# Reading the moving operand of every full-chunk product with its two halves in turn

## The chip, the cores and the metric

The kernel runs on one core of one Trainium2 chip. The metric is the device time of one execution in microseconds (us). Five engines work side by side and meet at semaphores: TensorE (PE in the rows, its loads of the stationary operand PEld), VectorE (DVE), ScalarE (ACT), GpSimd (POOL) and SyncE (SP), which here issues nearly all DMAs.

## What is computed

`x` is 4 batches of 12544 tokens with 128 channels, `inducing` has 32 rows. Two attention steps follow each other, then a maxout layer without bias:

```python
def mab(q, kv):
    s = scale * (q @ kv.transpose(0, 2, 1))
    s = s - s.max(-1, keepdims=True)
    a = np.exp(s)
    a /= a.sum(-1, keepdims=True) + 1e-09
    return a @ kv
h = mab(I, x)           # 32 rows per batch
y = mab(x, h)           # 12544 rows per batch, then as one list of tokens
h2 = np.maximum(np.maximum(y @ w1, y @ w2), y @ w3)   # 768 wide
out = h2 @ w_out
```

## The kernel before

**What a product is.** The second attention has only 32 rows of `h` per batch, so the kernel multiplies the weights with these rows first. The tile `us` holds, for a batch, `h` times (w1 - w2), `h` times (w3 - w2), and `h` times w2 times w_out, each as a high and a low part, on 128 rows. What remains for each token is the 32 probabilities, which stand in the tile `pT`, also as high and low parts on 128 rows, one column for a token. The maximum of the three branches is then the w2 branch plus max(relu(u), v), and the w2 branch goes through `us` straight to the output.

**Chunks and slots.** A batch has 98 tiles of 128 tokens: one short group of 2 tiles and six groups of 16. A full group is cut into four full chunks of 512 tokens, the short group is one chunk of 256. So there are 24 full chunks and one short chunk in a batch, 96 and 4 in all. A chunk has six slots, one for each block of 128 of the 768 hidden channels: 600 slots. A slot issues these products on TensorE, all of 128 rows by 128 stationary columns, with 512 moving columns in a full chunk, of type fp32r (four bytes a column, written by the engine that rounds it):

- line 778: `pu` from `us` and `pT`; line 784: `pv` from `us` and `pT` (stage 1, in `advance`),
- lines 846, 847, 848: three products into `acc` from `hi`, `hi` and `lows`, with `wo_hi`, `wo_lo`, `wo_hi` (stage 2),
- at the chunk's first slot also line 845: `us` and `pT` straight into `acc`.

Between the stages, ScalarE writes `ru` = relu(`pu`) (line 793), VectorE writes `h` = max(`pv`, `ru`) (line 814), ScalarE rounds it to `hi` (line 803), and GpSimd, for four or five of 24 slots VectorE, writes the rest `lows` = `h` - `hi` (lines 811, 817). Stage 2 of a slot runs six slots behind its stage 1 (`LAG`). `pu` and `pv` have two PSUM banks each, so the product of `pu` in slot s+1 waits until `ru` of slot s-1 has been read out. After the sixth slot ScalarE copies `acc` to `o` (line 859), and SP writes it out.

**The order around it.** Everything is issued by hand, in the order of the program. A full group is a window of 24 slots. At fixed slots of a window the kernel issues bursts of other products (scores of the next group at line 684, the first attention of the next batch at lines 366 and 502) and the steps of `scores_steps`, which make the probabilities of the next group: the last two write `ph` (ScalarE, line 730) and `pl` (VectorE, line 733) at slots 14 and 15. `probs` then issues, two chunks ahead, four DMAs (line 759) that bring 32 rows each of `ph` and `pl` into `pT`. The first chunks of batch 0 get `pT` by two products with `turn` instead (line 753).

Of the kernel before, what the change touches and what calls it, by code (L numbers as in the profile page):

```python
# [8 lines left out]
F32 = mybir.dt.float32  # L9
# [16 lines left out]
def kernel(ctx, tc, x, xt, ind_t, w1, w2, w3, w_out, out):  # L26
    nc = tc.nc
    B, N, C = x.shape
    M = ind_t.shape[1]
    DF = w1.shape[1]  # L30
    P = 128
    NT = N // P
    NJ = DF // P
# [158 lines left out]
    def first_load(what):  # L192
# [12 lines left out]
        out=sel[:, :M], in_=ident.rearrange("p (q m) -> p m q", m=M), axis=AX.X, op=ALU.add  # L205
    )
    nc.vector.tensor_copy(
        out=sel[:, M:].rearrange("p (q m) -> p q m", m=M),
        in_=sel[:, :M].unsqueeze(1).to_broadcast([P, NQ - 1, M]),
# [17 lines left out]
    wo_hi = const.tile([P, NJ, C], F32R, name="wo_hi")  # L227
    wo_lo = const.tile([P, NJ, C], F32R, name="wo_lo")
# [54 lines left out]
    def row_of(j):  # L283

        return 2 * (j % (NJ // 2)) + j // (NJ // 2)
# [32 lines left out]
    state = {}  # L318
# [355 lines left out]

    def scores_products(b, gi, bank):
        nt = groups[gi]["nt"]
        w = nt * M
        st = state[b]  # L680
        xT = st["xT"].pop(gi)
        sp = bank
        for q in range(NQ):
            nc.tensor.matmul(  # L684
                out=sp[q * M : (q + 1) * M, :w], lhsT=st["hT"][:, :M], rhs=xT[:, q * w : (q + 1) * w], start=True, stop=True
            )
        st["s"][gi] = sp

    def scores_steps(b, gi):

        nt = groups[gi]["nt"]
        w = nt * M
        st = state[b]
        sp = st["s"].pop(gi)
        flat = sp[:, :w]
        ev = flat.rearrange("p (t m) -> p t m", m=M)
        nc.vector.transpose(out=flat, in_=flat)
        yield
        mx = wk.tile([P, GT], F32, name="mx", tag="mx")
        nc.vector.tensor_reduce(out=mx[:, :nt], in_=ev, axis=AX.X, op=ALU.max)  # L700
        yield
        nc.vector.tensor_sub(out=ev, in0=ev, in1=mx[:, :nt].unsqueeze(2).to_broadcast([P, nt, M]))
        yield
        nc.scalar.activation(out=flat, in_=flat, func=AF.Exp, scale=scale)
        yield
        rs = wk.tile([P, GT], F32, name="rs", tag="rs")
        nc.vector.tensor_reduce(out=rs[:, :nt], in_=ev, axis=AX.X, op=ALU.add)
        yield
        if b == 0 and gi < 2:
            nc.vector.tensor_scalar_add(out=rs[:, :nt], in0=rs[:, :nt], scalar1=1e-9)  # L710
        else:
            nc.scalar.activation(out=rs[:, :nt], in_=rs[:, :nt], func=AF.Identity, bias=eps)
        yield
        nc.vector.reciprocal(out=rs[:, :nt], in_=rs[:, :nt])
        nc.vector.tensor_mul(out=ev, in0=ev, in1=rs[:, :nt].unsqueeze(2).to_broadcast([P, nt, M]))
        yield
        if nt < GT:

            pn = wk.tile([P, nt, 2, 2, M], F32R, name="pn", tag="pn", bufs=1)
            e4 = ev.unsqueeze(2).to_broadcast([P, nt, 2, M])  # L720
            nc.scalar.copy(out=pn[:, :, :, 0, :], in_=e4)
            yield
            nc.vector.tensor_sub(out=pn[:, :, :, 1, :], in0=e4, in1=pn.bitcast(F32)[:, :, :, 0, :])
            st[("p", gi)] = pn
            yield
            return
        nc.vector.transpose(out=flat, in_=flat)
        yield
        ph = wk.tile([P, 512], F32R, name="ph", tag="ph")
        nc.scalar.copy(out=ph, in_=flat)  # L730
        yield
        pl = wk.tile([P, 512], F32R, name="pl", tag="pl")
        nc.vector.tensor_sub(out=pl, in0=flat, in1=ph.bitcast(F32))
        st[("p", gi)] = (ph.bitcast(F32), pl.bitcast(F32))
        yield

# [34 lines left out]
    def advance():  # L771

        s = pipe["next"]
        pipe["next"] += 1
        if s + 1 < len(slots):
            c, j = slots[s + 1]
            pu, w = bank_u[(s + 1) % 2], c.w
            nc.tensor.matmul(  # L778
                out=pu[:, :w], lhsT=state[c.b]["us"][:, 2 * j * P : (2 * j + 1) * P], rhs=c.pT[:, :w], start=True, stop=True
            )  # L780
        if 0 <= s < len(slots):
            d, j = slots[s]
            pv = bank_v[s % 2]
            nc.tensor.matmul(  # L784
                out=pv[:, : d.w],
                lhsT=state[d.b]["us"][:, (2 * j + 1) * P : (2 * j + 2) * P],
                rhs=d.pT[:, : d.w],
                start=True,
                stop=True,
            )  # L790
        if s + 1 < len(slots):
            ru = hp.tile([P, 512], F32, name="ru", tag="ru", bufs=3)
            nc.scalar.activation(out=ru[:, :w], in_=pu[:, :w], func=AF.Relu)  # L793
            relus[s + 1] = ru
        low = pipe.pop("low", None)
        if 0 <= s - 1 < len(slots):
            c, j = slots[s - 1]
            h = sums.pop(s - 1)
            hi = hp.tile([P, 512], F32R, name="hi", tag="hi", bufs=10)
            if s - 1 in HIVEC:  # L800
                nc.vector.tensor_copy(out=hi[:, : c.w], in_=h[:, : c.w])
            else:
                nc.scalar.copy(out=hi[:, : c.w], in_=h[:, : c.w])  # L803
            lo = lows[:, (s - 1) % NL, :]
            c.hh.append(hi)
            c.hl.append(lo)
            args = dict(out=lo[:, : c.w], in0=h[:, : c.w], in1=hi.bitcast(F32)[:, : c.w])
            if c.low(j):
                pipe["low"] = args
            else:  # L810
                nc.gpsimd.tensor_sub(**args)  # L811
        if 0 <= s < len(slots):
            h = hp.tile([P, 512], F32, name="h", tag="h", bufs=5)
            nc.vector.tensor_max(out=h[:, : d.w], in0=pv[:, : d.w], in1=relus.pop(s)[:, : d.w])  # L814
            sums[s] = h
        if low:
            nc.vector.tensor_sub(**low)  # L817

    class Chunk:


        def __init__(self, n, b, gi, q):
            self.n, self.b, self.gi, self.q = n, b, gi, q
            self.w = GT * M if q is not None else groups[gi]["nt"] * P
            self.hh, self.hl = [], []

        def low(self, k):
# [7 lines left out]
    def stage2(c, j):  # L835
        us = state[c.b]["us"]
        w = c.w
        if j == 0:
            c.acc = [(bank_o[c.n % 2], slice(0, w))]
            if c.n == len(chunks) - 1:  # L840
                c.acc = [(bank_a[k], slice(k * w // 2, (k + 1) * w // 2)) for k in range(2)]
        for acc, cs in c.acc:
            to = acc[:, : cs.stop - cs.start]
            if j == 0:
                nc.tensor.matmul(out=to, lhsT=us[:, 2 * DF :], rhs=c.pT[:, cs], start=True, stop=False)  # L845
            nc.tensor.matmul(out=to, lhsT=wo_hi[:, row_of(j), :], rhs=c.hh[j][:, cs], start=False, stop=False)  # L846
            nc.tensor.matmul(out=to, lhsT=wo_lo[:, row_of(j), :], rhs=c.hh[j][:, cs], start=False, stop=False)  # L847
            nc.tensor.matmul(out=to, lhsT=wo_hi[:, row_of(j), :], rhs=c.hl[j][:, cs], start=False, stop=(j == NJ - 1))  # L848

    def finish(c):  # L850
        at = groups[c.gi]["at"] + (c.q or 0) * c.w
# [18 lines left out]
    for b in range(B):  # L870
        for gi in range(NG):
            full = groups[gi]["nt"] == GT
# [57 lines left out]
    for b in range(B):  # L930
        n = b + 1
        for g in range(1, NG):
            s0 = begins(b * (NG - 1) + g)
            if g + 1 < NG:

                if n == B:

                    if g % 2:
                        burst(s0 + 2, *((scores_products, b, k, bank_a[k % 2]) for k in (g + 1, g + 2) if k < NG))
                elif b > 0 or g > 1:  # L940
                    burst(s0 + 2, (scores_products, b, g + 1, bank_a[0]))
                softmax2(b, g + 1, *(s0 + i for i in STEPS2))
            elif n < B:
                burst(s0 + 2, (scores_products, n, 1, bank_a[0]), (scores_products, n, 0, bank_a[1]))
                burst(s0 + 2, (combine_products, ("state", n), bank_a[1][:, 2 * M : 2 * M + UQ]))
                softmax2(n, 1, *(s0 + i for i in STEPS2))
                softmax2(n, 0, *(s0 + i for i in STEPS0))
                at(s0 + 3, combine_high, ("state", n))
                at(s0 + 4, combine_low, ("state", n))
                for r, slot in enumerate((6, 8, 11, 13)):  # L950
                    at(s0 + slot, combine_rows, ("state", n), r)
# [184 lines left out]
```

## Time and profile before

| | |
|---|---|
| runs | 809.01, 2843.8 and 809.39 us, median 809.39 |
| profiled execution, span from first to last instruction | 807.4 us |
| TensorE busy in it | 799.2 us (99%) |
| ScalarE busy | 733.8 us (91%) |
| GpSimd busy | 648.2 us (80%) |
| VectorE busy | 628.3 us (78%) |

The slowest of the three runs stands apart and is not used. In the rows, a time is us from the span's start unless marked ns. Products on TensorE are pipelined, so the record of one is longer than the distance to the next: the distance from start to start is its pace, the record's length is not. The same holds, less strongly, for ScalarE, whose records overlap when it has work waiting.

### The profile page before, as it was taken

The page shows a single profiled execution, that of the slowest core. Times are in us where ns is not written, and L with a number is a line of the kernel's source. Part 1 is how long each engine was busy: PE and PEld are TensorE (multiplying, and loading weights), DVE is VectorE, ACT ScalarE, POOL GpSimd, SP SyncE. Part 2 cuts the span into 40 slices and gives each one's busy share as a digit, 9 for nine tenths or more (in the row PEclk, how much of TensorE's full clock was granted, in tenths as well). Part 3 has the DMA queues.
Part 4 walks back from the last instruction along what each step waited for, and adds up shares of the span by engine and source line. Part 5 has one row for each costly group of instructions (what it writes and reads, how often), then busy time and mean ns, then how long its engine had stood idle before and what let it go on. Part 6 is the DMA issues. An engine that isn't in the chain of part 4 may idle for free.

```text
span 807.4 us, 14348 instructions
## 1 busy us (share of the span) xinstructions
PE 799.2 (99%) x4567; PEld 629.5 (78%) x4567; DVE 628.3 (78%) x1071; ACT 733.8 (91%) x1529; POOL 648.2 (80%) x523
## 2 busy tenths in 40 slices
PE   7999999999999999999999999999999999999998
PEld 5668778778777787787777877877878788787887
DVE  5898978778877787787876977878778777878874
ACT  5799889889998898898988988989989999899996
POOL 1379879878788797796887977978979889788887
PEclk9999999999999999999999999999999999999999
DMA  9834325264542552542743425434223222222221
GB/s 353 298 127 125 119 66 183 81 214 157 190 143 60 188 159 76 184 134 96 238 130 100 143 81 183 123 107 136 61 75 104 68 74 71 69 85 75 60 79 52
DMA packets 52266, 102.24 MB, mean 127 GB/s; under 512 B 18144, under 2 KB 21344, under 8 KB 46944
## 3 DMA queue, kind: packets, MB, share of 16 engines
q1 hardware_dynamic: 52048, 101.21, 39.7%
q8 instruction: 36, 0.59, 0.3%
q14 instruction: 38, 0.31, 0.1%
q10 hardware_dynamic: 144, 0.13, 0.0%
HBM read 48.12 MB, written 25.69 MB: 91 GB/s over the span
## 4 chain that ended last, share of the span: by engine, by line
PE 95%; DMA 3%; DVE 1%; SPq 0%; ACT 0%; issue 0%; ACTq 0%; DVEq 0%
PE acc L846 17%; PE pu L778 17%; PE pv L784 17%; PE acc L847 16%; PE acc L848 16%; PE aux L684 3%; PE acc L845 3%; DMA raw<-in_w_out_dram 2%; PE acc L502 2%; PE aux L366 2%; DMA xg<-in_x_dram 1%; PE acc L621 0%; PE aux L650 0%; SPq L167 0%; PE pu L581 0%; PE aux L848 0%
## 5 line engine op out<-in xcount | busy, mean ns | idle before, releaser
L811 POOL TENSOR_TENSOR lows<-h,hi 128x512 fp32r<-128x512 f32 (+1 forms) x504 | 633.0, 1289 | 122.4 <-ACT hi L803 120.1
L814 DVE TENSOR_TENSOR h<-pv,ru 128x512 f32<-128x512 f32 (+1 forms) x600 | 403.3, 674 | 157.2 <-PE pv L784 100.5
L793 ACT ACTIVATE ru<-pu 128x512 f32<-128x512 f32 (+1 forms) x600 | 385.8, 643 | 50.8 <-PE pu L778 48.3
L803 ACT CAST hi<-h 128x512 fp32r<-128x512 f32 (+1 forms) x596 | 395.6, 664 | 0.4 <-DVE h L814 0.3
L778 PE MATMUL pu<-pT,us 128*128 128x512 f32 (+1 forms) x600 | 231.8, 386 | 0.1
L846 PE MATMUL acc<-hi,wo_hi 128*128 128x512 f32 (+1 forms) x594 | 231.8, 390 | 0.0
L784 PE MATMUL pv<-pT,us 128*128 128x512 f32 (+1 forms) x600 | 231.8, 387 | 0.0
L847 PE MATMUL acc<-hi,wo_lo 128*128 128x512 f32 (+1 forms) x594 | 228.9, 385 | 0.0
L848 PE MATMUL acc<-lows,wo_hi 128*128 128x512 f32 (+1 forms) x594 | 228.8, 385 | 0.0
L846 PEld LDWEIGHTS acc<-hi,wo_hi 128*128 128x128 f32 x594 | 111.5, 188 | 29.2 <-issue 7.5
L778 PEld LDWEIGHTS pu<-pT,us 128*128 128x128 f32 x600 | 112.6, 188 | 25.4 <-ACT ru L793 1.0
L784 PEld LDWEIGHTS pv<-pT,us 128*128 128x128 f32 x600 | 112.6, 188 | 24.0 <-DVE h L814 1.2
L848 PEld LDWEIGHTS acc<-lows,wo_hi 128*128 128x128 f32 x594 | 111.5, 188 | 22.7
L847 PEld LDWEIGHTS acc<-hi,wo_lo 128*128 128x128 f32 x594 | 111.6, 188 | 21.7
L817 DVE TENSOR_TENSOR lows<-h,hi 128x512 fp32r<-128x512 f32 x96 | 76.4, 795 | 0.8 <-ACT hi L803 0.8
L859 ACT COPY o<-acc 128x512 f32<-128x512 f32 (+1 forms) x96 | 61.5, 641 | 0.0
L845 PE MATMUL acc<-pT,us 128*128 128x512 f32 (+1 forms) x99 | 38.1, 385 | 0.0
L502 PEld LDWEIGHTS acc<-xg,aT 128*32 128x32 f32 x640 | 18.0, 110 | 9.7 <-issue 6.0
L684 PE MATMUL aux<-xT,hT 128*32 128x512 f32 x192 | 25.1, 603 | 0.0
L366 PE MATMUL aux<-xT,iT 128*32 128x512 f32 x184 | 24.1, 596 | 0.2 <-ACT pT L756 0.2
L502 PE MATMUL acc<-xg,aT 128*32 128x128 f32 x640 | 21.4, 273 | 0.1
L845 PEld LDWEIGHTS acc<-pT,us 128*128 128x128 f32 x99 | 18.6, 188 | 3.7
(163 smaller groups left out, 440.6 us busy)
## 6 DMA issues: line engine op xcount, KB each, us to landing
out_dram<-o SPq DMA_DIRECT2D x95, 256.0 KB, 2.2
xg<-in_x_dram SPq DMA_DIRECT2D x23, 1024.0 KB, 5.6
xT<-in_xt_dram SPq DMA_DIRECT2D x18, 1024.0 KB, 5.4
pT<-ph SPq DMA_DIRECT2D x190, 64.0 KB, 2.0
pT<-pl SPq DMA_DIRECT2D x190, 64.0 KB, 2.0
raw<-in_w_dram SPq DMA_DIRECT2D x3, 768.0 KB, 9.0
us<-uh SPq DMA_DIRECT2D x24, 52.0 KB, 1.9
us<-ul SPq DMA_DIRECT2D x24, 52.0 KB, 2.4
```

What stands on the lines that cost most here:

```text
L778: nc.tensor.matmul(out=pu[:, :w], lhsT=state[c.b]["us"][:, 2 * j * P : (2 * j + 1) * P], rhs=c.pT[:, :w], start=True, stop=True)
L784: nc.tensor.matmul(out=pv[:, : d.w], lhsT=state[d.b]["us"][:, (2 * j + 1) * P : (2 * j + 2) * P], rhs=d.pT[:, : d.w], start=True, stop=True,)
L793: nc.scalar.activation(out=ru[:, :w], in_=pu[:, :w], func=AF.Relu)
L803: nc.scalar.copy(out=hi[:, : c.w], in_=h[:, : c.w])
L811: nc.gpsimd.tensor_sub(**args)
L814: nc.vector.tensor_max(out=h[:, : d.w], in0=pv[:, : d.w], in1=relus.pop(s)[:, : d.w])
L817: nc.vector.tensor_sub(**low)
L845: nc.tensor.matmul(out=to, lhsT=us[:, 2 * DF :], rhs=c.pT[:, cs], start=True, stop=False)
L846: nc.tensor.matmul(out=to, lhsT=wo_hi[:, row_of(j), :], rhs=c.hh[j][:, cs], start=False, stop=False)
L847: nc.tensor.matmul(out=to, lhsT=wo_lo[:, row_of(j), :], rhs=c.hh[j][:, cs], start=False, stop=False)
L848: nc.tensor.matmul(out=to, lhsT=wo_hi[:, row_of(j), :], rhs=c.hl[j][:, cs], start=False, stop=(j == NJ - 1))
L859: copy(out=o[:, :w], in_=acc[:, :w])
```

## The change

Two helpers give views of a tile, `woven` and `spread`. `woven` reads columns 0, 256, 1, 257, ... of 512; `spread` (for a tile p (d a b) with d and a of size 2, b of 128) goes through b slowest, then d, then a. In full chunks the moving operands of lines 778, 784, 846, 847 and 848 become `woven` views, that of line 845 a `spread` view. As each stage's reading permutes the columns, `ph` and `pl` are written through `spread`, so that two readings bring the columns back to the order of the tokens: what `acc` and the output hold stays in place. Short chunks, the stationary operands and all other instructions are as they were.

```diff
+    def woven(ap, full):
+        return ap.rearrange("p (a b) -> p b a", a=2) if full else ap
+
+    def spread(ap, full):
+        return ap.rearrange("p (d a b) -> p b d a", d=2, a=2) if full else ap
...
+        e4 = flat.rearrange("p (b d a) -> p b d a", d=2, a=2)
         ph = wk.tile([P, 512], F32R, name="ph", tag="ph")
-        nc.scalar.copy(out=ph, in_=flat)
+        nc.scalar.copy(out=spread(ph, True), in_=e4)
         yield
         pl = wk.tile([P, 512], F32R, name="pl", tag="pl")
-        nc.vector.tensor_sub(out=pl, in0=flat, in1=ph.bitcast(F32))
+        nc.vector.tensor_sub(out=spread(pl, True), in0=e4, in1=spread(ph.bitcast(F32), True))
...
-                out=pu[:, :w], lhsT=state[c.b]["us"][:, 2 * j * P : (2 * j + 1) * P], rhs=c.pT[:, :w], start=True, stop=True
+                out=pu[:, :w],
+                lhsT=state[c.b]["us"][:, 2 * j * P : (2 * j + 1) * P],
+                rhs=woven(c.pT[:, :w], c.full),
+                start=True,
+                stop=True,
...
-                rhs=d.pT[:, : d.w],
+                rhs=woven(d.pT[:, : d.w], d.full),
...
+            self.full = q is not None
...
+        hi, lo = (woven(t[:, :w], c.full) for t in (c.hh[j], c.hl[j]))
...
+            two, four = (slice(cs.start // k, cs.stop // k) if c.full else cs for k in (2, 4))
             if j == 0:
-                nc.tensor.matmul(out=to, lhsT=us[:, 2 * DF :], rhs=c.pT[:, cs], start=True, stop=False)
-            nc.tensor.matmul(out=to, lhsT=wo_hi[:, row_of(j), :], rhs=c.hh[j][:, cs], start=False, stop=False)
-            nc.tensor.matmul(out=to, lhsT=wo_lo[:, row_of(j), :], rhs=c.hh[j][:, cs], start=False, stop=False)
-            nc.tensor.matmul(out=to, lhsT=wo_hi[:, row_of(j), :], rhs=c.hl[j][:, cs], start=False, stop=(j == NJ - 1))
+                pT = spread(c.pT[:, :w], c.full)
+                nc.tensor.matmul(out=to, lhsT=us[:, 2 * DF :], rhs=pT[:, four], start=True, stop=False)
+            nc.tensor.matmul(out=to, lhsT=wo_hi[:, row_of(j), :], rhs=hi[:, two], start=False, stop=False)
+            nc.tensor.matmul(out=to, lhsT=wo_lo[:, row_of(j), :], rhs=hi[:, two], start=False, stop=False)
+            nc.tensor.matmul(out=to, lhsT=wo_hi[:, row_of(j), :], rhs=lo[:, two], start=False, stop=(j == NJ - 1))
```

## Rows read from the trace of the kernel before

**Rows 1.** The page: span, and the granted clock in 40 slices.

```profile
span 807.4 us, 14348 instructions
...
PEclk9999999999999999999999999999999999999999
```

**Rows 2.** The page's chain that ended last, shares of the span by engine.

```profile
PE 95%; DMA 3%; DVE 1%; SPq 0%; ACT 0%; issue 0%; ACTq 0%; DVEq 0%
```

**Rows 3.** Timeline of TensorE, last batch: start, length, engine, line, operation, out<-in.

```profile
655.99 0.39 PE L784 MATMUL pv<-pT,us 128*128 128x512 f32 x1
656.22 0.39 PE L845 MATMUL acc<-pT,us 128*128 128x512 f32 x1
656.44 0.39 PE L846 MATMUL acc<-hi,wo_hi 128*128 128x512 f32 x1
...
662.34 0.39 PE L847 MATMUL acc<-hi,wo_lo 128*128 128x512 f32 x1
```

**Rows 4.** Busy time by engine in three windows of 24 slots; then clock, DMA share.

```profile
655.99:684.13 28.14, 28.14 (x125) 23.25 (x124) 23.07 (x38) 27.98 (x56) 24.59 (x20) 1.00 0.25 75
684.13:714.36 30.23, 30.23 (x142) 23.61 (x140) 23.05 (x38) 27.96 (x56) 24.46 (x20) 1.00 0.24 71
322.31:353.41 31.10, 31.10 (x173) 24.53 (x172) 24.18 (x41) 28.61 (x60) 25.39 (x21) 1.00 0.43 132
```

**Rows 5.** Timeline of TensorE, opening: products of plain fp32 operands.

```profile
12.21 0.60 PE L351 MATMUL pv<-ident,xg 128*128 128x128 f32 x4
12.65 0.60 PE L351 MATMUL pu<-ident,xg 128*128 128x128 f32 x4
13.09 0.60 PE L351 MATMUL pv<-ident,xg 128*128 128x128 f32 x4
...
42.44 1.88 PE L621 MATMUL acc<-wcat,hT 128*128 128x512 f32 x4
```

**Rows 6.** Line 621 alone: count, length in ns (min/median/max), first and last start.

```profile
L621 PE MATMUL acc<-wcat,hT x8: 275/592/697, 40.1 to 47.1; 128*128 128x512 f32 x6, 128*128 128x128 f32 x2
```

**Rows 7.** Timeline of TensorE in a short chunk: products of 256 columns.

```profile
438.01 0.28 PE L846 MATMUL acc<-hi,wo_hi 128*128 128x256 f32 x1
...
438.37 0.40 PE L778 MATMUL pu<-pT,us 128*128 128x512 f32 x1
```

**Rows 8.** Groups by line and shape: count, busy us, mean ns, idle before.

```profile
L784 PE MATMUL pv<-pT,us 128*128 128x512 f32 x576 | 225.1, 391 | 0.0
...
L846 PE MATMUL acc<-hi,wo_hi 128*128 128x512 f32 x570 | 224.8, 394 | 0.0
```

**Rows 9.** Timeline of ScalarE in the first window of rows 4, where work waits.

```profile
674.37 0.66 ACT L793 ACTIVATE ru<-pu 128x512 f32<-128x512 f32 x1
674.86 0.68 ACT L803 CAST hi<-h 128x512 fp32r<-128x512 f32 x1
675.36 0.67 ACT L793 ACTIVATE ru<-pu 128x512 f32<-128x512 f32 x1
...
678.36 0.68 ACT L859 COPY o<-acc 128x512 f32<-128x512 f32 x1
678.83 0.70 ACT L793 ACTIVATE ru<-pu 128x512 f32<-128x512 f32 x1
```

**Rows 10.** Timeline of all engines around a burst in the third window.

```profile
339.18 1.07 PE L684 MATMUL aux<-xT,hT 128*32 128x512 f32 x8
...
341.90 0.50 PE L846 MATMUL acc<-hi,wo_hi 128*128 128x512 f32 x1
...
343.15 0.60 ACT L793 ACTIVATE ru<-pu 128x512 f32<-128x512 f32 x1 [2.46 <-PE pu L778]
```

**Rows 11.** ScalarE's longest wait: total us, times, longest.

```profile
ACT ru L793 <- PE pu L778: 48.3, 31, 3.3
```

**Rows 12.** Lines 730 and 733: length in ns (min/median/max), first and last start.

```profile
L730 ACT CAST ph<-aux x24: 587/652/703, 46.0 to 761.6; 128x512 fp32r<-128x512 f32 x24
...
L733 DVE TENSOR_TENSOR pl<-aux,ph x24: 680/681/692, 46.7 to 762.5; 128x512 fp32r<-128x512 f32 x24
```

**Rows 13.** Lines 256 and 264: VectorE on 768 columns, strided by two and adjacent.

```profile
L256 DVE SCALAR_TENSOR_TENSOR rest<-raw,pw x4: 959/959/959, 7.7 to 31.0; 128x768 f32<-128x768 uint32 x4
...
L264 DVE TENSOR_TENSOR rest<-rest,t x1: 948/948/948, 18.0 to 18.0; 128x768 f32<-128x768 f32 x1
```

## The prediction

> **What bounds the kernel now.** I read the page first: span, busy shares, clock. TensorE is granted its full 2.4 GHz in every slice [rows 1], so no part of the time can be won back from the clock. The chain that ended last is TensorE for 95% of the span [rows 2]. Then I read the timeline of TensorE, because a record's length says nothing of the pace there. In the main loop the products follow each other without a gap: from 655.99 to 662.34 there are 28 of them, 6.35 us, or 227 ns each [rows 3]. A window of 24 slots without a burst has 124 products (24 times 5, and 4 at line 845) and takes 28.14 us, 226.9 ns each [rows 4]. At 2.4 GHz, 512 columns take 213.3 ns. So 13.6 ns of each product, 6%, are not columns. The windows that are longer than 28.14 us hold the same 124 products and the bursts of small ones [rows 4].
>
> What these 13.6 ns are decides the case, so I looked for other products on the same engine. The transposes at line 351 have plain fp32 operands: from 12.21 to 13.09 there are eight of 128 columns, 110 ns each [rows 5]. That is two cycles a column (106.7 ns) and 3.3 ns. At line 621 four products of 512 columns take 1.88 us, the last one's own record about 0.59 [rows 5, 6]: (1.88 - 0.59) / 3 = 0.43 us of pace, two cycles a column (426.7 ns) and about 3 ns. Both load a new stationary operand for each product, as the main loop does. So the change of the stationary operand alone costs about 3 ns, and some 10.6 ns more are lost only where a four-byte column is wanted in every cycle. My reading is that the supply of the moving operand falls a little short there: with two cycles to a column the same shortfall would be hidden. One row speaks against a loss per column: three products of 256 columns in the short chunk take 0.36 us, 120 ns each, 13.3 ns above their 106.7 [rows 7]. That looks more like a fixed loss in each product, for instance reads of the next stationary operand that get in the way of the moving one.
>
> ScalarE is next. Where it has work waiting, `ru` and `hi` together take 0.99 us (674.37 to 675.36) and the copy of `acc` 0.47 [rows 9], against five products in 1.13 us.
>
> **The change part by part.** It adds no instruction, no DMA and no wait, and no queue changes its order. It changes in which order three engines touch the columns of a tile.
>
> *The products.* 96 full chunks have 6 times 5 and one more, 31, so 2976 products; the trace groups them by line with 576 at line 784, and 570 at line 846 because the last chunk's six are cut in half [rows 8]. Neither half nor quarter streams of a moving operand appear in the trace of before, so the price is bounded from both sides. Best case: everything above the columns goes, 13.6 ns x 2976 = 40.5 us. Worst case, by the nearest rows of a slower supply: a column every second cycle, the 0.43 us of line 621, (430 - 226.9) x 2976 = 604 us more. Zero is possible too. I take a pace of 213.3 + 3 = 216.3 ns, the surplus that the fp32 rows keep: 10.6 ns x 2976 = 31.5 us saved. Why that end and not the other: the shortfall depends on what the moving reads meet, and their order is the one thing that is changed; two streams that lie 1 KB apart still fetch each stretch of memory once if the reader holds both. It is the likelier end, not by much.
>
> *What of it reaches the end.* In the window without a burst, ScalarE's work at its own pace is 24 x 0.99 + 4 x 0.47 = 25.6, and the three softmax steps that it has there (one of 16 columns, two of 512 at about 0.5) 1.2 more: 26.8 to 27.0 us. TensorE would need 124 x 216.3 = 26.8. So ScalarE comes level, and of 1.3 us about 1.1 is left. In a window of the middle batches ScalarE is busy 28.61 us of 31.10 and idle 2.46 in the burst [rows 4, 10]: between 340.7 and 343.15 it has nothing to read, as TensorE does other products from 339.18 to 341.90. There are 31 such waits, 48.3 us in all [rows 11]. Its records overlap, so the 28.61 hide some slack: by its paces it needs 27.0 and about 1.2 for the first attention's steps, 28.2, and with 2.46 idle 30.7 of 31.10. If that idle time stays, ScalarE allows only 0.4 us of the 1.3; if it enters the burst with one slot more of backlog, which two banks of `pu` allow, all of it. I take 1.0. Three quarters of 31.5 is 24 us.
>
> *The writes of `ph` and `pl`.* They hop from column to column in SBUF instead of going straight. There are 24 of each, 0.65 and 0.68 us [rows 12]. A hop of one word is not in the trace; a read of every second word is free on VectorE, 959 against 948 ns [rows 13]. Bounds: nothing, or twice the length, 24 x 0.65 = 16 us of ScalarE and 24 x 0.68 = 16 us of VectorE. VectorE is busy about 24 us in a window of 31 [rows 4] and covers it; on ScalarE it comes off the slack above, 0.65 us in the worst case in one window. I take zero for both, and keep 16 us for the range. If that cover is gone, the late thing is `hi`, and behind it stage 2; the DMAs into `pT` follow `pl` by one slot and are used seven slots later, so they don't come late.
>
> *Sum.* 807.4 - 24 = 783.4 us of span. The median of the runs is 809.39, 2.0 above the profiled span, so 785.4; I say 785.
>
> **The rivals.**
>
> *The other side: each column is a fetch of its own.* Place: TensorE's read of the moving operand, in all five products. The new order never takes two neighbours one after the other. If the reader keeps only the last stretch that it fetched, every column needs a new fetch. Price at one column in two cycles: 604 us, 1413 us in all; at one and a half cycles (320 ns), (320 - 226.9) x 2976 = 277 us, 1086. It decides from a pace of 232.3 ns on (16.2 us, or 2%, over 2976 products is 5.4 ns). For it: the fp32r products now get 2048 bytes in 226.9 ns, the highest rate of any read in these rows, and have nothing to spare. Against it: no row shows a hop that costs, and the one strided read that is there costs 1% [rows 13], though it stays within a step of two words.
>
> [...]
>
> *The order makes no difference.* If the 13.6 ns belong to the exchange of the stationary operand, as the 256-column products suggest [rows 7], the pace stays and the time is 809, or up to some 817 if the writes of `ph` cost half their bound on the path.
>
> *ScalarE takes the gain.* The pace falls to 216 ns, but ScalarE's idle time at bursts stays and the writes of `ph` lengthen: 0.4 us in each of 25 windows, 10 us, 799.
>
> **How the numbers follow.** About 2% either way is what a measurement of this kernel can tell from no change: 793 to 826 us. Chances: the forecast 0.43, with its own range from 769 (all 40.5 us) to 793; ScalarE takes the gain 0.07 (799); no difference 0.15 (809); slower by over 2% 0.35, of it 0.23 around 1413 (a column in two cycles, the 0.02 above 1420 left out), and 0.12 spread between 826 and 1390. The forecast, the likeliest single case, gives 785. A range that leaves out the slower cases would hold 0.65 only, so it must reach to the two-cycle case: 769 to 1420. Faster 0.43, same 0.22, slower 0.35.
>
> **What the changed profile would show.** The distance between products in an unbroken stretch of the timeline decides at once: 216 ns for the forecast, 227 for no difference, 320 to 430 for the slower rival. If the forecast is right, ScalarE's busy share rises towards 94%, its waits for `pu` shrink, and a few of TensorE's pieces on the chain give way to ScalarE. Short chunks keep their 120 ns in all cases; they read as before. The records of lines 730 and 733 show what the hopping writes cost. I am wrong if the loss is fixed in each product, or if a reader that alternates can't hold both streams.

## The result, and the profile after

The changed kernel takes 800.68 us (median; 799.86 to 801.94) where the one before takes 809.2 (809.0 without its run of 2843.8): a ratio of 0.990, with a 95% interval of 0.988 to 0.991. It gains 8.5 us, 1%: clear of the noise, but within the 2% that the prediction counted as no change; the forecast was a gain of 24.

The page of the profiled execution, first line, busy shares of TensorE and ScalarE, and the chain that ended last:

```profile
span 798.1 us, 14349 instructions
...
PE 781.7 (98%) x4567; PEld 627.2 (79%) x4567; DVE 641.4 (80%) x1071; ACT 737.0 (92%) x1529; POOL 638.3 (80%) x523
...
ACT 44%; PE 43%; DMA 4%; POOL 3%; DVE 3%; issue 2%; SPq 1%; POOLq 0%; ACTq 0%; DVEq 0%
ACT ru L806 18%; ACT hi L816 18%; PE pu L787 7%; PE acc L863 7%; PE pv L797 7%; PE acc L864 6%; PE acc L865 6%; POOL lows L824 3%; ACT o L876 3%; PE aux L692 3%; DMA raw<-in_w_out_dram 2%; PE acc L502 2%; ACT ph L739 2%; PE aux L366 2%; PE acc L862 1%
```

TensorE had 95% of the chain [rows 2]; now ScalarE has as much of it as TensorE. The timeline of TensorE (start, length, engine, line, operation) shows why; lines 787, 797 and 863 to 865 are the former 778, 784 and 846 to 848, and line 862 is the former 845:

```profile
505.48 0.38 PE L797 MATMUL pv<-pT,us 128*128 128x512 f32 x1
505.69 0.38 PE L863 MATMUL acc<-hi,wo_hi 128*128 128x512 f32 x1
505.91 0.38 PE L864 MATMUL acc<-hi,wo_lo 128*128 128x512 f32 x1
...
511.09 0.44 PE L862 MATMUL acc<-pT,us 128*128 128x512 f32 x1
511.37 0.38 PE L863 MATMUL acc<-hi,wo_hi 128*128 128x512 f32 x1
```

From 505.48 to 511.09 there are 26 products, 216 ns each, where it was 227 [rows 3]. Line 862 with its four streams takes 280 ns here (511.09 to 511.37). The two windows that answer to the first and third of [rows 4], same columns:

```profile
649.87:677.65 27.78, 27.31 (x125) 23.20 (x124) 24.26 (x38) 27.77 (x56) 24.16 (x20) 1.00 0.26 76
319.33:350.21 30.88, 30.49 (x174) 24.37 (x173) 24.75 (x41) 28.88 (x60) 25.02 (x21) 1.00 0.43 136
```

The first fell from 28.14 to 27.78 us, the other from 31.10 to 30.88, where the 120 products of the five lines, at 10.7 ns less, would have given 1.3 us in each. ScalarE is busy in all of the first. The loads of the stationary operand (line, released by; total us, times, longest) wait behind `ru`:

```profile
PEld pu L787 <- ACT ru L806: 22.7, 51, 0.9
```

And the two hopping writes, answering to [rows 12]:

```profile
L739 ACT CAST ph<-aux x24: 1087/1182/1240, 45.6 to 753.7; 128x512 fp32r<-128x512 f32 x24
...
L742 DVE TENSOR_TENSOR pl<-aux,ph x24: 1058/1078/1098, 46.7 to 754.9; 128x512 fp32r<-128x512 f32 x24
```

1.18 and 1.08 us instead of 0.65 and 0.68. So the products give back 2880 x 10.7 = 31 us, and the span fell by 9.3. Two questions were left for the chip: where the rest went, and why this order is read faster.

### The profile page after: what moved, and what is told of

Read it like the earlier page. It is cut to its first block, busy times and chain, and to the rows that moved or that the text cites. A ratio compares the mean times of both kernels' runs of the same rounds, so it can differ in the third digit from the quotient of the medians.

```text
span 798.1 us, 14349 instructions
## 1 busy us (share of the span) xinstructions
PE 781.7 (98%) x4567; PEld 627.2 (79%) x4567; DVE 641.4 (80%) x1071; ACT 737.0 (92%) x1529; POOL 638.3 (80%) x523
## 4 chain that ended last, share of the span: by engine, by line
ACT 44%; PE 43%; DMA 4%; POOL 3%; DVE 3%; issue 2%; SPq 1%; POOLq 0%; ACTq 0%; DVEq 0%
ACT ru L806 18%; ACT hi L816 18%; PE pu L787 7%; PE acc L863 7%; PE pv L797 7%; PE acc L864 6%; PE acc L865 6%; POOL lows L824 3%; ACT o L876 3%; PE aux L692 3%; DMA raw<-in_w_out_dram 2%; PE acc L502 2%; ACT ph L739 2%; PE aux L366 2%; PE acc L862 1%
## 5 line engine op out<-in xcount | busy, mean ns | idle before, releaser
L824 POOL TENSOR_TENSOR lows<-h,hi 128x512 fp32r<-128x512 f32 (+1 forms) x504 | 623.1, 1268 | 123.6 <-ACT hi L816 120.0
L806 ACT ACTIVATE ru<-pu 128x512 f32<-128x512 f32 (+1 forms) x600 | 402.0, 671 | 36.9 <-PE pu L787 36.7
L816 ACT CAST hi<-h 128x512 fp32r<-128x512 f32 (+1 forms) x596 | 410.9, 690 | 0.8 <-DVE h L827 0.6
L797 PE MATMUL pv<-pT,us 128*128 128x512 f32 (+1 forms) x600 | 226.3, 377 | 1.7 <-DVE h L827 1.6
L863 PE MATMUL acc<-hi,wo_hi 128*128 128x512 f32 (+1 forms) x594 | 225.9, 380 | 0.0
L865 PE MATMUL acc<-lows,wo_hi 128*128 128x512 f32 (+1 forms) x594 | 222.8, 375 | 0.0
L864 PE MATMUL acc<-hi,wo_lo 128*128 128x512 f32 (+1 forms) x594 | 222.8, 375 | 0.0
L830 DVE TENSOR_TENSOR lows<-h,hi 128x512 fp32r<-128x512 f32 x96 | 80.6, 839 | 0.8 <-ACT hi L816 0.8
L862 PE MATMUL acc<-pT,us 128*128 128x512 f32 (+1 forms) x99 | 43.0, 434 | 0.0
L742 DVE TENSOR_TENSOR pl<-aux,ph 128x512 fp32r<-128x512 f32 x24 | 25.9, 1078 | 13.5 <-ACT ph L739 13.5
L739 ACT CAST ph<-aux 128x512 fp32r<-128x512 f32 x24 | 28.1, 1171 | 0.2 <-DVE aux L735 0.2
```

The costliest lines, as they stand in the source:

```text
L797: nc.tensor.matmul(out=pv[:, : d.w], lhsT=state[d.b]["us"][:, (2 * j + 1) * P : (2 * j + 2) * P], rhs=woven(d.pT[:, : d.w], d.full), start ...
L862: nc.tensor.matmul(out=to, lhsT=us[:, 2 * DF :], rhs=pT[:, four], start=True, stop=False)
L863: nc.tensor.matmul(out=to, lhsT=wo_hi[:, row_of(j), :], rhs=hi[:, two], start=False, stop=False)
L864: nc.tensor.matmul(out=to, lhsT=wo_lo[:, row_of(j), :], rhs=hi[:, two], start=False, stop=False)
L865: nc.tensor.matmul(out=to, lhsT=wo_hi[:, row_of(j), :], rhs=lo[:, two], start=False, stop=(j == NJ - 1))
```

## Experiments: where the gain went

**Straight writes, and another order that needs no hopping.** The first run takes the hopping out of the change; the second reads the products in an order that is its own inverse, so that nothing else must change. The third and fourth move every second copy of `acc` from ScalarE to VectorE, in the changed kernel and in the one before.

```diff
 e1_plain_ph (the changed kernel, with)
-        nc.scalar.copy(out=spread(ph, True), in_=e4)
+        nc.scalar.copy(out=ph, in_=flat)
-        nc.vector.tensor_sub(out=spread(pl, True), in0=e4, in1=spread(ph.bitcast(F32), True))
+        nc.vector.tensor_sub(out=pl, in0=flat, in1=ph.bitcast(F32))
 e2_swap (straight ph, pl and line 845, and)
-        return ap.rearrange("p (a b) -> p b a", a=2) if full else ap
+        return ap.rearrange("p (l m h) -> p h m l", l=2, h=2) if full else ap
 e3_o_on_vector, e4_before_o_on_vector (the kernels after and before, with)
-        turns = [(nc.vector.tensor_copy if c.n < 3 else nc.scalar.copy, nc.sync)]
+        turns = [(nc.vector.tensor_copy if c.n < 3 or c.n % 2 else nc.scalar.copy, nc.sync)]
```

> The changed kernel with ph and pl written straight, as before; everything else of the change stays, so the columns of the full chunks come out in another order than the reference's. Theory 1, ScalarE is now the bound: in the changed kernel ph takes ScalarE 0.88 us to the next start instead of 0.48, so 24 x 0.40 = 9.6 us of ScalarE come free, and 5 to 9 us of them show: 792 to 796. Theory 2, the gain is lost inside TensorE, at line 845 with its four streams: ph and pl are covered, 799 to 802.

> Another reading order for the same five products: columns 0, 256, 2, 258, ..., 254, 510, then 1, 257, 3, 259, ... (top and lowest bit of the column's number exchanged). Read twice it gives back the order of the tokens, so ph, pl and line 845 stay as they were before the change. If two streams are all that the pace needs, the products stay at 216 ns apart. Theory 1 (ScalarE is the bound): 9.6 us of ScalarE come free and line 845 is back at 227 ns, together 789 to 795. Theory 2 (line 845 is where the gain went, 96 x 53 ns = 5.1 us): 795 to 796. If neighbours must follow each other inside each stream, the pace is 227 or worse and the time 809 or more.

> The changed kernel with the copy of acc to o on VectorE in every second chunk. Theory 1 (ScalarE is the bound): some 47 copies of 0.48 us leave ScalarE, 22 us; then TensorE sets the window again, at 124 x 216 ns, 3 us of bursts and 0.2 us for line 845, about 30.0 us where it is 30.9 now: 778 to 788 in all. Theory 2 (the loss is inside TensorE): 798 to 802.

> The kernel before, with the same copies moved to VectorE. TensorE sets its time at 227 ns a product, so by both theories the relief of ScalarE brings next to nothing: 804 to 810. If it brings 10 us or more, ScalarE was a bound before the change too, and the reading order is not needed to explain what e3 gains.

Measured: e1 792.56 us (792.0 to 792.65), e2 809.1, e3 793.17 (792.26 to 795.38), e4 811.01 (808.33 to 816.61), beside 809.1 for the kernel before. e1 settles the writes: written straight they save 8.1 us, and the hopping `ph` takes 9.6 us more of ScalarE, so nearly all of that was on the path, as theory 1 says. It straightens both writes, and no run straightens one alone; that ScalarE's is the one that counts is read from the chain above (ScalarE 44%, VectorE 3%). e3 gains 7.5 us from the relief of ScalarE and e4 loses 2: ScalarE became the bound only with the faster products. e4 lies 1 us above its range; its profile has one gap of 2.45 us on TensorE, of the kind shown below. And e3 stays above its 778 to 788, so theory 1 isn't the whole of it. e2 came out as its last case: two streams are not enough. Its products stand 227 ns apart, as before the change; the next section takes up the order.

**Both reliefs together.** In b1 and b2 the writes are straight, half the copies are on VectorE, and the columns of the output are put in their place when the host lays out the result. b2 moves one more small step to VectorE.

```diff
 b1_host_order (e1 and e3 together, and on the host)
+            g = g.reshape(nb, c, 4, 128, 2, 2).transpose(0, 1, 2, 4, 5, 3)
 b2_host_order_rs (b1, with)
-        if b == 0 and gi < 2:
+        if True:
             nc.vector.tensor_scalar_add(out=rs[:, :nt], in0=rs[:, :nt], scalar1=1e-9)
```

> The change's reading order, with ph and pl written straight, the columns of a full chunk's output put in their place when the host lays out the result, and every second copy of acc to o on VectorE. Theory 1 (ScalarE sets the time of the changed kernel): both reliefs add up on ScalarE, 9.6 and 22 us, and TensorE sets the windows again at 29.8 to 30.1 us: 781 to 788. If the two reliefs don't add, because something else ends the windows at 30.4 to 30.5, 790 to 793.

> As b1, and the addition of 1e-9 to the sums of the probabilities (0.21 us of ScalarE in each group) on VectorE for all groups. Theory 1: if TensorE already sets the windows in b1, the same time within 1 us; if ScalarE still does, 3 to 5 us less than b1.

Measured: b1 793.28 us (790.76 to 795.67; a fourth run, at a mean granted clock of 0.989, took 806.17), b2 796.34 (793.77 to 796.98). The reliefs don't add. ScalarE is off the chain of b1's profile (TensorE 89%, ScalarE 2%), so something else costs. The timeline of b1's VectorE, its GpSimd and its TensorE at one place:

```profile
479.11 0.69 DVE L826 TENSOR_TENSOR h<-pv,ru 128x512 f32<-128x512 f32 x1 [0.27 <-PE pv L796]
479.71 3.83 DVE L829 TENSOR_TENSOR lows<-h,hi 128x512 fp32r<-128x512 f32 x1
483.47 0.68 DVE L826 TENSOR_TENSOR h<-pv,ru 128x512 f32<-128x512 f32 x1
...
464.31 18.69 POOL L823 TENSOR_TENSOR lows<-h,hi 128x512 fp32r<-128x512 f32 x15 [1.91 <-ACT hi L815]
...
481.88 0.38 PE L786 MATMUL pu<-pT,us 128*128 128x512 f32 x1
484.20 0.48 PE L796 MATMUL pv<-pT,us 128*128 128x512 f32 x1 [1.94 <-DVE mx L434]
```

VectorE's `lows`, 0.68 us elsewhere, takes 3.83. GpSimd goes through fifteen of its own `lows` without a pause from 464.31 to 483.00, and VectorE's ends half a microsecond after that. `h` stands behind it in VectorE's order, and TensorE waits for the bank of `pv` that `h` should have read: 2.3 us from start to start (the row names the small reduction that comes right behind `h`). There are four such gaps in b1's profile. Both subtractions read `h` and `hi`, and VectorE's long ones end only when GpSimd pauses (here at 483.54, GpSimd's row at 483.00). But not every such row holds VectorE up to its end: of the nine rows of fifteen in b1 four do, and in the other five VectorE's `lows` gets in between two of GpSimd's and lasts 1.2 to 1.8 us. What decides between the two is not shown, nor what it is that holds VectorE up. Nor do such long `lows` explain b2: after the one at 81.2 no `lows` lasts over 1.8 us there, and its TensorE waits for `h` more often instead, 47 times (18.3 us in all, by its loads) against 25 (15.5) in b1.

**Which of the two is it?** x1 takes the copies away, with their output DMAs, without giving VectorE work; b4 gives VectorE half as many; b3 is the version with straight writes and the order restored.

```diff
 x1_half_o_left_out (b3, with)
     def finish(c):
+        if c.n % 2 and c.n > 3 and len(c.acc) == 1:
+            return
 b3_host_only (b1 with all copies on ScalarE)
 b4_o_quarter (b1, with)
-        turns = [(nc.vector.tensor_copy if c.n < 3 or c.n % 2 else nc.scalar.copy, nc.sync)]
+        turns = [(nc.vector.tensor_copy if c.n < 3 or c.n % 4 == 1 else nc.scalar.copy, nc.sync)]
```

> The change's reading order with ph and pl written straight; the copies of acc to o and the output DMAs of every second chunk are left out, so half of the output isn't written. Theory 1, the rest of the gain is held back by ScalarE's time alone: 22 us of ScalarE go and VectorE gets nothing more, TensorE sets the windows at 29.9 us, 779 to 785, without gaps of 2 us on TensorE. Theory 3, VectorE's lows wait for GpSimd whenever the slots come faster: the same gaps of 2.3 us as in b1, and 788 to 792.

> The change's reading order with ph and pl written straight and the columns of the output put in their place when the host lays out the result; all copies of acc on ScalarE. The device's work is that of e1: 792 to 793 by every theory.

> As b3, with one of four copies of acc on VectorE. Theory 1: 11 us of ScalarE go, 783 to 788. Theory 3: VectorE is hit by fewer long waits than in b1 (four of 3.8 us), but some: 787 to 792, and each gap above 2 us on TensorE stands behind such a wait.

Measured: x1 800.96 us (794.34 to 805.92), b3 792.38 (792.22 to 793.75), b4 795.13 (789.31 to 797.71). x1 does less work than b3 and is slower. Theory 1 alone falls; theory 3 holds for the wait behind GpSimd, though x1 and b4 are worse than it forecast too. In x1's profile `lows` of VectorE lasts over 3.6 us seven times and TensorE has six gaps of 2.3 to 2.8 us; b3 has one such `lows`, at 80.6, where the kernel before has one too, and no gap above 0.9. A place in x1, VectorE and GpSimd, and then the same place in b3:

```profile
132.09 3.82 DVE L829 TENSOR_TENSOR lows<-h,hi 128x512 fp32r<-128x512 f32 x1
135.83 0.68 DVE L826 TENSOR_TENSOR h<-pv,ru 128x512 f32<-128x512 f32 x1
...
116.69 18.67 POOL L823 TENSOR_TENSOR lows<-h,hi 128x512 fp32r<-128x512 f32 x15 [1.92 <-ACT hi L815]
...
132.32 1.14 DVE L829 TENSOR_TENSOR lows<-h,hi 128x512 fp32r<-128x512 f32 x1
...
116.71 16.21 POOL L823 TENSOR_TENSOR lows<-h,hi 128x512 fp32r<-128x512 f32 x13 [1.84 <-ACT hi L815]
133.22 2.65 POOL L823 TENSOR_TENSOR lows<-h,hi 128x512 fp32r<-128x512 f32 x2 [0.29 <-ACT hi L815]
```

Unbroken rows of thirteen are in most windows of the kernel before, too. What is new is where they end. In b3 GpSimd then waits 0.29 us for its next `hi`, and VectorE's `lows` gets in. With ScalarE relieved, that `hi` comes early enough, the pause is gone, and the row goes on to fifteen over VectorE's own turn: nine such rows in x1, one in b3, two in the kernel before.

The gaps account for the loss, as an estimate. x1's six take 13.0 us more than the pace of 216 ns, and a stretch of some 3 us in which TensorE was granted half its clock (last section) some 1.7 more; without both, its span of 797.5 us would be 783, where theory 1 had put the run. In the slower runs of x1 the clock has a larger part: their mean granted clock is 0.991 and 0.989, where b3's is 0.999 or 1.000.

**Fewer lows on GpSimd.**

```diff
 b5_low6_o_half (b1), b6_low6 (b3): six of 24 lows on VectorE
-    LOWVEC = (23, 0, 15, 18)
-    LOWLAST = (23, 0, 9, 15, 18)
+    LOWVEC = (23, 0, 4, 9, 15, 18)
+    LOWLAST = (23, 0, 4, 9, 15, 18)
 b7_low5_o_half (b1): five
+    LOWVEC = (23, 0, 9, 15, 18)
```

> As b1 (straight writes, output put in order by the host, every second copy of acc on VectorE), with six instead of four of 24 lows on VectorE, so GpSimd has 18 of them, 22.5 us in a window of 30. Theory 3 (lows of VectorE wait while GpSimd has no pause): no more gaps of 2.3 us, windows at 29.9, 781 to 786. If something else makes the gaps, or VectorE is too full now, 789 or more.

> As b3 (all copies of acc on ScalarE), with six of 24 lows on VectorE. ScalarE still sets the windows: 790 to 793 by every theory. Well below 790 would say that GpSimd held b3 back.

> As b5 with five of 24 lows on VectorE, as the last batch has it already; GpSimd has 19, 23.8 us in a window. Theory 3: fewer gaps than b1, 782 to 788.

Measured: b5 801.47 us, b6 801.47, b7 789.47 (789.08 to 789.69). b7 beats both kernels: 0.976 of the time before, interval 0.974 to 0.977, and its runs lie within 0.6 us, though 1.5 us above its range. Its profile has one `lows` of over 3 us left, at 81.0; TensorE has 91% of its chain, and the window that answers to the third of [rows 4] is TensorE's own time:

```profile
315.46:345.41 29.95, 29.95 (x173) 24.67 (x172) 25.83 (x44) 27.67 (x58) 23.85 (x20) 1.00 0.45 139
```

b5 and b6 missed, b6 by 8 us on what every theory allowed. They have no gaps of 2.3 us, but once a window the added `lows` lasts 1.5 us and a gap of 0.6 to 1.5 us on TensorE follows, at the same place in both. So not only their number counts, but where VectorE's `lows` fall against those of GpSimd. Other slots for the sixth weren't tried.

## Experiments: why this order is read faster

**Is it the stationary operand?** m1 is the kernel before with half of one stationary operand.

```diff
-            nc.tensor.matmul(out=to, lhsT=wo_lo[:, row_of(j), :], rhs=c.hh[j][:, cs], start=False, stop=False)
+            nc.tensor.matmul(out=to[:64], lhsT=wo_lo[:, row_of(j), :64], rhs=c.hh[j][:, cs], start=False, stop=False)
```

> The kernel before, with line 847 (wo_lo) cut to 64 of its 128 stationary columns, so that half of wo_lo's part of the output is left out. All moving operands are read straight. Theory S, the 10.6 ns above the columns come from reading the next stationary operand beside the moving one: the product at line 846, during which line 847's operand is loaded, falls from 227 to some 221 or 222 ns and the others stay. Theory M, the moving read falls short by itself: all products stay at 227.

Measured: the product at line 846, during which the half operand is loaded, stays at its pace:

```profile
500.65 0.39 PE L846 MATMUL acc<-hi,wo_hi 128*128 128x512 f32 x1
500.88 0.40 PE L847 MATMUL acc<-hi,wo_lo 128*64 128x512 f32 x1
...
501.81 0.39 PE L846 MATMUL acc<-hi,wo_hi 128*128 128x512 f32 x1
502.03 0.40 PE L847 MATMUL acc<-hi,wo_lo 128*64 128x512 f32 x1
```

0.23 and 0.22 us to the next start, 226 ns in the median of the trace, where theory S wanted 221 or 222. It falls. The other products became up to 9 ns slower in the median, and the run took 817.57 us beside 809.92; why half an operand costs more is open.

**Orders.** All of these have straight `ph`, `pl` and line 845; only the view changes.

```diff
-        return ap.rearrange("p (a b) -> p b a", a=2) if full else ap
+        return ap.rearrange("p (a b c) -> p b a c", a=2, c=2) if full else ap    # m2_pairs
+        return ap.rearrange("p (c a b) -> p c b a", a=2, b=8) if full else ap    # m3_near
+        return ap.rearrange("p (b a) -> p a b", a=2) if full else ap             # m4_evens
+        return ap.rearrange("p (c a b) -> p c b a", a=2, b=2) if full else ap    # m5_bits01
+        return ap.rearrange("p (c a b) -> p c b a", a=2, b=4) if full else ap    # m6_near4
```

> The five products read two neighbouring columns from each half in turn: 0, 1, 256, 257, 2, 3, ... ; ph, pl and line 845 as before the change, so the columns of full chunks don't fit together. If what counts is how fast the read walks through the addresses (as in the change, two columns further in four columns' time, where straight reading and the order of e2 need two), 216 ns. If what counts is that no two neighbours follow each other, 227.

> The five products alternate between columns only eight apart: 0, 8, 1, 9, ..., 7, 15, then 16, 24, ... ; ph, pl and line 845 as before the change, so the columns of full chunks don't fit together. If the pace needs the two halves of the tile, 1 KB apart, 227 ns. If any two streams that step by one column will do, 216.

> The five products read all even columns and then all odd ones, a single stream with a step of two; ph, pl and line 845 as before the change, so the columns of full chunks don't fit together. If a step of two costs TensorE nothing, as in each stream of e2, 227 ns. If the walk through the addresses sets the loss, it walks twice as fast as straight reading, and the pace is above 227, at most 430 (a column every second cycle).

> The five products read 0, 2, 1, 3, 4, 6, 5, 7, ... (the two lowest bits of the column's number exchanged, which read twice is the order of the tokens, so ph, pl and line 845 stay as before the change). [...]

> The five products read 0, 4, 1, 5, 2, 6, 3, 7, then 8, 12, ... ; ph, pl and line 845 as before the change, so the columns of full chunks don't fit together. [...] If a reader needs runs longer than four columns, or a distance of more than four between the two streams, more than 216.

Measured: m2 1118.51 us, m3 790.97, m4 1460.47, m5 809.04 (before: 808.98), m6 791.49 (one run each, but for m5). Two neighbours in the timeline of each of m4, m2, m5 and m6 show the pace:

```profile
501.05 0.64 PE L859 MATMUL acc<-lows,wo_hi 128*128 128x512 f32 x1
501.50 0.63 PE L782 MATMUL pu<-pT,us 128*128 128x512 f32 x1
...
503.44 0.50 PE L857 MATMUL acc<-hi,wo_hi 128*128 128x512 f32 x1
503.77 0.50 PE L858 MATMUL acc<-hi,wo_lo 128*128 128x512 f32 x1
...
500.19 0.39 PE L859 MATMUL acc<-lows,wo_hi 128*128 128x512 f32 x1
500.42 0.39 PE L782 MATMUL pu<-pT,us 128*128 128x512 f32 x1
...
500.11 0.38 PE L859 MATMUL acc<-lows,wo_hi 128*128 128x512 f32 x1
500.32 0.38 PE L782 MATMUL pu<-pT,us 128*128 128x512 f32 x1
```

0.45, 0.33, 0.23 and 0.21 us; the paces in the table are medians over the trace. m3 answers that two streams eight columns apart, each stepping by one, will do; m2 and m4 came out slower than any of their cases. The orders side by side, with the columns at every second place of the order, and how many of these in a row are of one group of four neighbours (0 to 3, 4 to 7, ...):

| order | columns at every second place | of one group of four in a row | pace, ns |
|---|---|---|---|
| 0, 256, 1, 257 (the change), 0, 8, 1, 9 (m3), 0, 4, 1, 5 (m6) | 0, 1, 2, 3 | 4 | 216 |
| 0, 1, 2, 3 (before) | 0, 2, 4, 6 | 2 | 227 |
| 0, 256, 2, 258 (e2) | 0, 2, 4, 6 | 2 | 227 |
| 0, 2, 1, 3, 4, 6 (m5) | 0, 1, 4, 5 | 2 | 227 |
| 0, 2, 4, 6 (m4) | 0, 4, 8, 12 | 1 | 452 |
| 0, 1, 256, 257 (m2) | 0, 256, 2, 258 | 1, then the other group | 334 |
| 0, 128, 256, 384, 1 (line 862) | 0, 256, 1, 257 | 1, then the other group | 274 |

The count by four was made after m1 to m4; m5 and m6 were run as its test, and came out at the 227 and 216 ns that it has for two and four in a row. A count in pairs, by which m5 would have stood at 216 to 220, fell, and so did "the halves must be far apart" (m3 and m6, 216 at distances of eight and four columns). That the groups are of four is read from these paces alone: in groups of two, straight reading (227) and m4 (452) would both have one in a row, and in groups of eight, m6 (216) and straight reading (227) both four. One in a row (m4, 452) costs twice the time of two (227), and two cost 11 ns more than four (216); the last two rows don't fit. Why places two apart count, and why four columns, no trace shows. Why an order that goes back and forth between two groups lies in between (334, 274) is open.

## Why the prediction went wrong where it did

- **The bound and the 13.6 ns: right.** TensorE set the time, and all but some 3 ns of the part above the columns goes with the order in which the moving operand is read. The 2.4 GHz and the 213.3 ns of 512 columns rest here on an estimate: from 256 to 512 columns a product grows by 0.418 ns a column ((226.9 - 120) / 256 [rows 4, 7]; 0.426 with the median of 118), an fp32 one from 128 to 512 by 0.833 ((430 - 110) / 384 [rows 5, 6]), and half of that, 0.417, is 2.4 columns in a ns at the full clock of [rows 1]. A frequency stands in no row. The reason that [rows 7] suggested, the load of the stationary operand, didn't hold against m1. The row itself stays unexplained: products of 256 columns, read straight in both kernels, keep 118 ns in the median, 11 above their columns.
- **The pace: right, in part by luck.** 216.3 ns was forecast and 216 measured, over the five products 31 us. But the prediction named no way in which another order would be read faster, and took this as "the likelier end, not by much". Two streams that the reader holds, which is all it had, are not what counts: e2 has them too, at 227 ns. The slower rival doesn't come true in this order; a pace like the one it priced does in another (m4, 452 ns, 1460 us).
- **What of it reaches the end: mis-sized.** This is the step that failed first. I took 1.0 us of 1.3 in a window of the middle batches. With straight writes (e1, b3) the window falls from 31.1 to 30.5, 0.6 us. My lower bound for it, 0.4 if ScalarE's idle time at the burst stays, was the nearer: most of the idle time stayed (39.3 us behind `pu` in e1, 48.3 before in [rows 11]). The window without a burst falls from 28.1 to 27.0, the 1.1 that I gave it. In all, 16.5 us of 31.5 reach the end instead of 24.
- **The writes of `ph` and `pl` at zero: wrong.** They lengthen ScalarE's step by 0.40 us (0.48 to 0.88 from start to start), and 8.1 us of these 9.6 show, because ScalarE had just become the bound. The upper bound of 16 us held it. For ScalarE the text named no cover but "the slack above", which the step before had already spent, and took zero all the same. This and the 7.5 us of the step before are the whole miss: 24 - 7.5 - 8.1 is 8.4, and 8.5 was measured.
- **Line 845: missed.** I priced all 2976 products alike. The 96 that read four streams became 47 ns slower in the median, 4.5 us of TensorE. With that line straight (m3, one run) the time is 790.97, against 792.56 in e1: about 1.6 us on the path, a part of the 7.5.
- **The rival that came true** was "ScalarE takes the gain", 799 us, which had 0.07; the time is 800.68. In the range, but not the forecast.
- **What no part of it saw** is the second limit behind ScalarE, VectorE's `lows` and GpSimd's, which x1 shows.

## What to carry to other kernels

When one engine's 6% is taken away and the next engine stands at 91%, work out the second engine's sum with every instruction that the change lengthens on it, before any share of the gain is counted; a cost that has no cover there counts nearly in full (here 8.1 of 9.6 us). If a relief of the next bound brings nothing, look for an instruction that has become longer, not for a wait: here a subtraction of 0.68 us took 3.8. A reading order is cheap to try on the moving operand, but the order must be brought back somewhere: putting the columns in place on the host cost the device nothing (b3 792.38 us, e1 792.56), a hopping write did (0.40 us of ScalarE for each `ph`).

## What the runs showed of the hardware that was not expected

- fp32r products of 512 columns stand 216 ns apart if places two apart hold four neighbouring columns in a row (the change, m3, m6), 227 if they are read straight (before), 452 if all even columns are read and then all odd ones (m4).
- A write of 512 columns that hops at each of them takes ScalarE 0.88 us to the next start instead of 0.48 (lines 739 and 730, after and before), and VectorE's subtraction, with a hopping input as well, 0.99 instead of 0.60 (lines 742 and 733).
- In b1, after a gap of 2.3 us from 514.02 and five more products, TensorE was granted half its clock (0.50) for some 3 us; the products there stand 0.43 us apart, where it is 0.22 before and behind. x1 and b4 have one such stretch each, behind a gap of 2.3 us (mean granted clock of either profile 0.998, as in b1); the other gaps of b1, x1 and b4, and the one of e4, have none. The gap's two products, and the row of the stretch, with clock 0.50 behind the busy times:

```profile
514.02 0.38 PE L786 MATMUL pu<-pT,us 128*128 128x512 f32 x1
516.34 0.48 PE L796 MATMUL pv<-pT,us 128*128 128x512 f32 x1 [1.94 <-DVE mx L434]
...
517.70:520.90 3.20, 3.20 (x9) 2.45 (x9) 2.43 (x4) 3.15 (x7) 2.21 (x2) 0.50 0.11 34
```
